# Nyström attention and two MoE layers on one core: the Newton turns of both head groups as one alternating product, and later scores

## The chip, the cores and the metric

One core of a Trainium2 chip. The metric is the device time of one execution in microseconds, on which PE (TensorE), DVE (VectorE), ACT (ScalarE), POOL (GpSimd), SP (SyncE) and the DMA queues work side by side. Each engine takes its instructions in order. The kernel before took 835.98 us (median of 3 runs, 835.73 to 837.34).

## The reference, cut to what matters

```python
B, H, S, D = q.shape            # 4, 8, 576, 64
m = 32
q_lm, k_lm = means of 18 rows of q, k          # 32 landmarks
A  = softmax(q @ k_lm.T / 8)                   # 576 x 32
Bm = softmax(q_lm @ k_lm.T / 8)                # 32 x 32
C  = softmax(q_lm @ k.T / 8)                   # 32 x 576
Z = Bm.T / (norm_1(Bm) * norm_inf(Bm) + 1e-06)
for _ in range(6):
    Z = 2 * Z - Z @ Bm @ Z                     # six Newton turns
x = A @ Z @ C @ v                              # per batch and head, then 2304 x 512
x = silu(x @ w_in) @ w_out                     # MoE1, d_ff 2048
xn = rms_norm(x) * rms_g
return (silu(xn @ w_gate) * (xn @ w_val)) @ w_out2   # MoE2, d_ff 1536
```

Everything is in fp32.

## The kernel before

**The order of the work.** Batch 0's attention comes first (`head`, in an order written out by hand). MoE1 then runs in 128 steps, 32 for each batch: two halves `hf` of 288 tokens, 16 blocks `f` of 128 hidden columns. The attention of batches 1 to 3 runs beside the MoE1 steps of the batch before it. MoE2 follows in three blocks of 768 tokens. A tile framework turns the order in which the code is traced, together with priorities, into one instruction list for each engine, with semaphores for the data and for the reuse of buffers.

**A step of MoE1.** `moe1_h` (L1018) makes `h`, 128 x 288, by six matmuls of 288 columns (products of a high and a low part), ACT makes `s` = silu(h), and ACT and DVE split `s` into the two parts of `hl` (L164, L165). `moe1_out` multiplies `hl` by `wo` into four accumulators `a` (L1038, 12 matmuls). Batch 0 takes unsplit `s` and `wor` in most of its steps (L1035, four fp32 matmuls). `retire` calls `moe1_out` three steps after its `h`. When a half is done, `moe1_sum` adds the four `a` to what is stored (`e`, L1063, DVE). During batch 0's steps DVE and ACT also turn `w_out` into its split form: `wor` (L189, L191) and `wo` (L165), 512 columns at a time. W' = `w_in` x the batch's small matrix is made in `wprime` (`pw`, L849).

**The attention of a batch.** The eight heads are two groups `g` of four heads, and a head has 32 of the 128 partitions. `attention(ap, b, g)` is a generator; each MoE1 step advances it by one `yield` (two in steps 20 to 31). Its stages are: loads of q and k; `landmarks`, a DVE sum of 128 x 1152 elements for each of `qT` and `kT` (L200); `scores` (16 matmuls, `pq` and `c`, each on a tile of 64 rows and 32 columns, L267); the maxima, exponentials and `bb` (Bm); `p1` (products and norms of Bm); `ct` (five transposes of C, L288); `pu` (C @ v, L295, 40 records of fp32); the six turns; `pl` (L828). Between them the query softmax `sa` is transposed to `sb` and split into `at` (`key_part`).

**A turn.** State `rt` is 128 x 96: 32 columns of R, made from Z Bm - I, and 64 of U. A turn needs R @ [R, U]:

```python
for it in range(6):
    pe_ = ps(f"pe_{n}_{it}", [P, 96])
    blocks(pe_[:, lo:], rt[:, 0:M], rt[:, lo:], start=True, stop=True)
    VE.tensor_copy(r2[:, 0:M], pe_[:, 0:M])
    VE.tensor_tensor(y, rt[:, M:], pe_[:, M:], op=ALU.add if it else ALU.subtract)
    yield
```

`blocks` (L273) issues four matmuls of 32 x 32 x 96 for the four heads, each on the tile (h, h) of the array: rows of head h, columns of head h. Both groups use the same four tiles. The last turn computes the 64 columns of U alone (`ud`). `head` gives batch 0 another form, in which a second product by plus or minus the identity adds U on PE and one copy empties the sum.

Group 0 runs LONE = 5 steps ahead of group 1. All PSUM tiles but the accumulators (`h`, scores, `p1`, `ct`, `pu`, `pe`, `pl`, `pw`) share four banks, `ps`. After batch 3's attention `att` is closed and pool `p2` opens, in which the first jobs of MoE2 (`pre`) work.

Of the kernel before, what the change touches and what calls it, by code (L numbers as in the profile page):

```python
# [10 lines left out]
F32 = mybir.dt.float32  # L11
F32R = mybir.dt.float32r
# [66 lines left out]
LOW = 9  # L79
LONE = 5  # L80


@with_exitstack
def nystrom_moe_kernel(ctx: ExitStack, tc: tile.TileContext, q, k, v, w_in, w_out, w_gate, w_val, w_out2, rms_g, out):
# [63 lines left out]
    def ps(name, shape=(P, 512)):  # L148
        return pr.tile(list(shape), F32, tag="r", name=name)
# [519 lines left out]
    def attention(ap, b, g):  # L669
# [40 lines left out]
        yield  # L710
        if b > 1:
            yield

        sa = ht("sa", [P, R, M])
        w1 = 320
        c1 = ps(f"c1_{n}", [P, w1])
        c2 = ps(f"c2_{n}", [P, S + M - w1])
        for hf, ci, lo, hi in ((0, c2, w1, S + M), (1, c1, 0, w1)):
            pq = ps(f"pq_{n}_{hf}", [P, HB])
            with tc.issue_after(h_mm[0].ins):  # L720
                for i in range(2):
                    scores(qT, kT, i, pq, ci, HB * hf, HB * hf + HB, lo, hi)
            VE.transpose(sa[:, 9 * hf:9 * hf + 9].rearrange("p r j -> p (r j)"), pq)
# [29 lines left out]
        VE.tensor_scalar(bb[:, 0], bb[:, 0], rc[:, 1:2], None, op0=ALU.mult)  # L753
        VE.transpose(bb[:, 1], bb[:, 0])
# [14 lines left out]
        ct = big("ct", [P, 5, P])  # L769
        tps = []  # L770
        for (i0, i1) in ((0, 4), (4, 5)):
            tp = ps(f"ct_{n}_{i0}", [VC[i0], i1 - i0, P])
            turn(tp, ec, i0, i1)
            tps.append((i0, i1, tp))
        yield
# [10 lines left out]
        VE.reciprocal(rc[:, 0:1], rc[:, 0:1])  # L786
        VE.tensor_scalar(rt[:, M:96], pu, rc[:, 0:1], ic, op0=ALU.mult, op1=ALU.mult)
        VE.tensor_tensor(sa, sa, msb, op=ALU.mult)
        yield
        keys = 0  # L790

        def key_part():
            nonlocal sb, at, keys
            if keys == 0:
                sb = big("sb", [P, S])
                VE.transpose(sb, sa.rearrange("p r j -> p (r j)"))
            elif keys == 1:
                at = xp.tile([P, 2, S], F32R, tag="x", name=f"at_{n}")
                AE.copy(at[:, 0], sb)
            elif keys == 2:  # L800
                VE.tensor_tensor(at[:, 1], sb, at[:, 0].bitcast(F32), op=ALU.subtract)
                at_t[b, g] = at
            keys += 1

        sb = at = None
        if g == 0:
            for _ in range(LONE):
                key_part()
                yield
        for it in range(6):  # L810
            pe_ = ps(f"pe_{n}_{it}", [P, 96])
            lo = 0 if it < 5 else M
            blocks(pe_[:, lo:], rt[:, 0:M], rt[:, lo:], start=True, stop=True)
            if it == 5:
                ud = mt("ud", [P, D])
            y = r2[:, M:] if it < 5 else ud
            if it < 5:
                VE.tensor_copy(r2[:, 0:M], pe_[:, 0:M])
            VE.tensor_tensor(y, rt[:, M:], pe_[:, M:], op=ALU.add if it else ALU.subtract)
            rt, r2 = r2, rt  # L820

            if it:
                key_part()
            yield

        hr = slice(64 * g, 64 * g + 64)
        pl = ps(f"pl_{n}", [P, 4, M])
        PE.matmul(pl[hr].rearrange(fl, h=4), ud, bbd.rearrange(fl, h=4), start=True, stop=True)  # L828
        if b not in lts:
            lts[b] = st.tile([P, 4, M], F32, tag="lt", name=f"lt_{b}", bufs=2)  # L830
        VE.tensor_copy(lts[b][hr], pl[hr])
        l_t[b, g] = True

# [320 lines left out]
    def store_out(e, row, last):  # L1154

        for h in range(2):
            y = slice(64 * h, 64 * h + 64)
            (SP, POOL, ACT)[h and last].dma_start(out=out[row + 64 * h:row + 64 * h + 64], in_=e[y])

# [84 lines left out]
    def out_tile(prev, n):  # L1244
# [9 lines left out]
        if f == NF2 - 1:  # L1254
            e = nslot(n, f"e2_{p}_{n}", [P, DM])
            last = 0 if p < NB2 // 2 - 1 else 1 + n // 5
            if last < 2:
                (DVE.tensor_copy if n % 2 else ACT.copy)(e, oacc[n])
            else:
                DVE.tensor_copy(e[:, :DM // 2], oacc[n][:, :DM // 2])  # L1260
                ACT.copy(e[:, DM // 2:], oacc[n][:, DM // 2:])
            store_out(e, (2 * p + j) * TB + t * P, last)

# [34 lines left out]
    VE.last, AE.last = Queue.last[DVE], Queue.last[ACT]  # L1298

    def behind(ins, fn):  # L1300
        with ExitStack() as es:
            for x in ins:
                es.enter_context(tc.issue_after(x.ins))
            fn()

# [54 lines left out]
    for i, (b, hf, f, c) in enumerate(steps):  # L1360
# [24 lines left out]
        if b == 0:  # L1385
# [129 lines left out]
```

## Time and profile before

| | us |
|---|---|
| median of 3 runs | 835.98 (835.73 to 837.34) |
| the profiled execution | 836.19 |
| its span in the trace | 834.1 |
| PE busy | 820.4 (98%) |
| DVE busy | 530.7 (64%) |
| ACT busy | 441.1 (53%) |

The span is what the trace shows between the first and the last instruction; 2.1 us of the execution lie around it. A row of a timeline gives the start in the span, the time from the first instruction's start to the last one's end, the line, the operation, what it writes and reads, tile and shape, and the number of records. An fp32 matmul leaves two records. The ends of matmuls overlap the next starts, so the time of a run is read from its start to the next row's start.

### The profile page before, as it was taken

The numbers are of one execution on the slowest core, as the hardware profiler recorded it, in microseconds if no ns is written. First come the engines' busy times: TensorE is split into PE (matmuls) and PEld (weight loads), VectorE is DVE, ScalarE is ACT, GpSimd is POOL, SyncE is SP. The second block draws the span as 40 slices with busy tenths as digits, with TensorE's granted clock in tenths as the row PEclk, the third lists the DMA queues.
The fourth block names the chain that finished last, engine by engine and source line by source line (L and its number), as shares of the span: only waits on it lengthen the run. The fifth ranks groups of instructions, "written<-read, shape, count | busy, mean of one in ns | idle before, by whom it ended". The sixth has DMA issues, their size and how long they took to land.

```text
span 834.1 us, 15381 instructions
## 1 busy us (share of the span) xinstructions
PE 820.4 (98%) x5912; PEld 734.1 (88%) x5912; DVE 530.7 (64%) x1141; ACT 441.1 (53%) x929; POOL 15.6 (2%) x45
## 2 busy tenths in 40 slices
PE   8899999999999999999999999999999999999997
PEld 5577677998898989999999999999999999999996
DVE  6988878786688767779735489543558433233323
ACT  4786755785668757775534456433245323233222
POOL 2200000000000000000000000000000000000001
PEclk9999999999999999999999999999999999999999
DMA  9989457458894679989975458678456557665542
GB/s 343 352 299 367 151 171 259 129 191 281 309 321 156 200 269 350 337 292 317 330 287 214 166 191 299 228 239 299 187 222 227 189 181 274 227 227 193 182 192 76
DMA packets 73320, 202.85 MB, mean 243 GB/s; under 512 B 6720, under 2 KB 34880, under 8 KB 69280
## 3 DMA queue, kind: packets, MB, share of 16 engines
q1 hardware_dynamic: 72928, 201.09, 67.2%
q8 instruction: 47, 0.77, 0.4%
q0 software_dynamic: 240, 0.66, 0.3%
q14 instruction: 25, 0.20, 0.1%
q10 hardware_dynamic: 80, 0.13, 0.0%
HBM read 149.29 MB, written 52.56 MB: 242 GB/s over the span
## 4 chain that ended last, share of the span: by engine, by line
PE 93%; ACT 2%; DMA 2%; DVE 1%; issue 1%; SPq 0%; POOL 0%; POOLq 0%; DVEq 0%; ACTq 0%
PE a L1038 21%; PE ga L1179 18%; PE o L1253 18%; PE h L1018 12%; PE gc L1179 9%; PE gb L1179 5%; PE a L1035 4%; PE pw L849 2%; DMA wor<-in_moe_w_out_dram 1%; PE pe L273 1%; DMA qT<-in_q_dram 1%; PE pu L295 1%; PE pq L267 1%; PE c L267 0%; PE ct L288 0%
## 5 line engine op out<-in xcount | busy, mean ns | idle before, releaser
L1038 PE MATMUL a<-hl,wo 128*128 128x288 f32 x1296 | 195.5, 299 | 1.2 <-DVE e L1063 1.2
L1038 PEld LDWEIGHTS a<-hl,wo 128*128 128x128 f32 x1296 | 177.8, 188 | 8.3 <-issue 2.9
L1253 PE MATMUL o<-oc,u 128*128 128x512 f32 x648 | 178.9, 394 | 0.0
L1179 PE MATMUL ga<-x,w 128*128 128x384 f32 x840 | 170.9, 338 | 0.0
L1179 PEld LDWEIGHTS ga<-x,w 128*128 128x128 f32 x840 | 151.3, 188 | 12.3 <-ACT a L200 0.2
L1253 PEld LDWEIGHTS o<-oc,u 128*128 128x128 f32 x648 | 119.4, 188 | 13.6 <-DVE u L165 0.3
L1018 PE MATMUL h<-at,wp 128*128 128x288 f32 x768 | 128.6, 302 | 0.0
L1018 PEld LDWEIGHTS h<-at,wp 128*128 128x128 f32 x768 | 109.6, 188 | 14.0 <-issue 5.9
L200 DVE TENSOR_TENSOR v<-u,gc 128x384 f32<-128x384 f32 x72 | 39.7, 551 | 122.6 <-PE gc L1179 122.1
L1179 PE MATMUL gc<-x,w 128*128 128x384 f32 x420 | 84.8, 336 | 0.0
L1025 ACT ACTIVATE s<-h 128x288 f32<-128x288 f32 x108 | 44.1, 412 | 74.8 <-PE h L1018 74.7
L1179 PEld LDWEIGHTS gc<-x,w 128*128 128x128 f32 x420 | 75.0, 188 | 2.9
L200 ACT COPY u<-ga 128x384 f32<-128x384 f32 x72 | 34.5, 480 | 72.9 <-PE ga L1179 72.6
L200 DVE TENSOR_TENSOR u<-z,v 128x384 f32<-128x384 f32 x72 | 40.1, 557 | 46.6 <-ACT z L200 45.5
L164 ACT CAST u<-u 128x384 fp32r<-128x384 f32 x72 | 37.0, 514 | 61.1 <-DVE u L200 61.0
L165 DVE TENSOR_TENSOR hl<-s,hl 128x288 fp32r<-128x288 f32 x108 | 49.1, 455 | 20.9 <-ACT hl L164 20.3
L165 DVE TENSOR_TENSOR u<-u,u 128x384 fp32r<-128x384 f32 x72 | 40.1, 557 | 26.3 <-ACT u L164 26.0
L200 ACT ACTIVATE z<-ga 128x384 f32<-128x384 f32 x36 | 17.7, 492 | 68.9 <-PE ga L1179 68.6
L164 ACT CAST hl<-s 128x288 fp32r<-128x288 f32 x108 | 46.6, 434 | 2.7
L1035 PE MATMUL a<-s,wor 128*128 128x288 f32 x160 | 42.6, 410 | 0.9 <-issue 0.9
L1179 PE MATMUL gb<-x,w 128*128 128x384 f32 x210 | 42.4, 336 | 0.0
L1035 PEld LDWEIGHTS a<-s,wor 128*128 128x128 f32 x160 | 29.1, 189 | 11.1 <-issue 3.3
(218 smaller groups left out, 931.1 us busy)
## 6 DMA issues: line engine op xcount, KB each, us to landing
w<-w7d SPq DMA_DIRECT2D x31, 1792.0 KB, 7.3
oc<-wod SPq DMA_DIRECT2D x32, 512.0 KB, 7.8
win<-wind SPq DMA_DIRECT2D x20, 512.0 KB, 5.3
w2d<-c SPq DMA_DIRECT2D x36, 256.0 KB, 2.5
fw<-w2d SPq DMA_DIRECT2D x12, 768.0 KB, 7.0
winr<-in_moe_w_in_dram SPq DMA_DIRECT2D x8, 1024.0 KB, 8.1
wor<-in_moe_w_out_dram SPq DMA_DIRECT2D x16, 512.0 KB, 9.8
w7d<-w7p SPq DMA_DIRECT2D x16, 512.0 KB, 5.1
```

The lines of the kernel that those rows point to most:

```text
L164: x = ACT.copy(dst[:, 0], src) if hi is ACT else hi.tensor_copy(dst[:, 0], src)
L165: return x, lo.tensor_tensor(dst[:, 1], src, dst[:, 0].bitcast(F32), op=ALU.subtract)
L200: self.last = getattr(self.eng, name)(*args, **kw)
L267: eng.matmul(out[32 * o:32 * o + 32], lm[y, i, S:], t[y, i, x0:x1], start=True, stop=True)
L273: eng.matmul(out[o], x[o], y[o], **kw)
L849: PE.matmul(pw[g][32 * i:32 * i + 32], lts[b][hr, i], win_t[i // 2, nb_][hr, i % 2], start=True, stop=True)
L1018: h_mm[0] = PE.matmul(ph, w[:, x, fo:fo + P], a[:, y, tk], start=i == 0, stop=i == 5)
L1025: ACT.activation(s, ph, AF.Silu)
L1035: PE.matmul(acc[d], w[:, y], hl, start=start, stop=stop)
L1038: PE.matmul(acc[d], w[:, x, y], hl[:, z], start=start and i == 0, stop=stop and i == 2)
L1179: mm[0] = PE.matmul(acc, w7[:, x, o, kk], xs[:, y, kk], start=start and n == 0, stop=stop and n == 5, skip_group_check=True)
L1253: PE.matmul(oacc[n], hls[j][:, x, t * P:(t + 1) * P], w[:, y], start=f == 0 and i == 0, stop=f == NF2 - 1 and i == 2)
```

## The change

1. `attend(ap, b)` takes the place of the two generators in the main loop and drives both. Group 0 starts `LONE[b]` steps ahead: 6, 8, 8 for batches 1, 2, 3. The extra yields before the scores are 0, 2, 1 (0, 1, 1 before). The turns begin when both groups have their `rt`.
2. A turn is one run of 16 matmuls, chained in order. The first eight multiply R by `rt` (96 columns, 64 in the last turn) and the other eight add U by plus or minus the identity (64 columns) into the same PSUM tile. The groups alternate: group 0 on tile (h, h), group 1 on tile (h, h^1). One DVE copy per group empties a turn. That makes 144 matmuls more and 36 DVE operations in place of 66 in three batches.
3. The 16 matmuls of a group's scores are chained as one run. `ct` comes before `p1` in another chain, behind the transpose of `bb`. `sb` and `at` are made before the turns, each at its own yield. `pl` of both groups is one run, and its copy has the sign.
4. The last output tile: DVE and ACT copy the halves into two tiles, which leave as 128 rows of 256 columns on POOL's and ACT's queues. Before, both wrote one tile, stored as 64 rows each by SP and ACT.

```diff
-LONE = 5
+LONE = (0, 6, 8, 8)
...
     class Queue:
         last = {}
-        def __init__(self, eng):
+        def __init__(self, eng, last=None):
             self.eng = eng
+            self.last = Queue.last if last is None else last
...
                     if self.eng in self.last:
                         es.enter_context(tc.issue_after(self.last[self.eng].ins))
+                        if self.last is not Queue.last:
+                            es.enter_context(tc.high_priority(offset=PU_PRIO))
...
-        if b > 1:
+        for _ in range((0, 0, 2, 1)[b]):
             yield
...
+        run = Queue(PE, {})
...
-                    scores(qT, kT, i, pq, ci, HB * hf, HB * hf + HB, lo, hi)
+                    scores(qT, kT, i, pq, ci, HB * hf, HB * hf + HB, lo, hi, run)
...
-        blocks(p1[:, 0:M], bb[:, 1], bb[:, 1], start=True, stop=True)
-        PE.matmul(p1[:, M:], ones_bd.rearrange(fl, h=4), bb.rearrange("p t j -> p (t j)"), start=True, stop=True)
+        run = Queue(PE, {})
+        tps = []
+        for (i0, i1) in ((0, 4), (4, 5)):
+            tps.append((i0, i1, ps(f"ct_{n}_{i0}", [VC[i0], i1 - i0, P])))
+        with behind([last]):
+            for i0, i1, tp in reversed(tps):
+                turn(tp, ec, i0, i1, run)
+            blocks(p1[:, 0:M], bb[:, 1], bb[:, 1], run, start=True, stop=True)
+            run.matmul(p1[:, M:], ones_bd.rearrange(fl, h=4), bb.rearrange("p t j -> p (t j)"), start=True, stop=True)
...
+    def attend(ap, b):
+        gens = [attention(ap, b, g) for g in range(NG)]
+        for _ in range(LONE[b]):
+            next(gens[0])
+            yield
+        while len([x for x in newton if x[0] == b]) < NG:
+            for gn in gens:
+                next(gn, None)
+            yield
+        rs = [list(x) for x in rts]
+        ins = [newton[b, g][1] for g in range(NG)]
         for it in range(6):
...
+            pes = [ps(f"pe_{b}_{g}_{it}", [P, 96]) for g in range(NG)]
+            run = Queue(PE, {})
+            for x0, x1, x, start in ((lo, 96, None, True), (M, 96, id32 if it else nid32, False)):
+                for h in range(4):
+                    for g, (rt, r2) in reversed(list(enumerate(rs))):
+                        y, z = slice(32 * h, 32 * h + 32), slice(32 * (h ^ g), 32 * (h ^ g) + 32)
+                        with behind(ins):
+                            run.matmul(pes[g][z, x0:x1], (rt[:, 0:M] if x is None else x)[y], rt[y, x0:x1], start=start, stop=not start, skip_group_check=True)
+            ins = []
+            for g, r in enumerate(rs):
+                if it == 5:
+                    r[1] = ap.tile([P, D], F32, tag="m", name=f"ud_{b}_{g}", bufs=7)
+                    ins.append(VE.tensor_copy(r[1], pes[g][:, M:]))
+                else:
+                    ins.append(VE.tensor_copy(r[1], pes[g]))
+                r.reverse()
+                next(gens[g], None)
             yield
...
+                e2 = nslot(n + 1, f"e2_{p}_{n}_1", [P, DM])
+                half = DM // 2
+                for eng, fn, t, x in ((POOL, DVE.tensor_copy, e, slice(0, half)), (ACT, ACT.copy, e2, slice(half, DM))):
+                    fn(t[:, x], oacc[n][:, x])
+                    eng.dma_start(out=out[row:row + P, x], in_=t[:, x])
...
-            gens = [attention(ap, nxt, g) for g in range(NG)]
+            gens = [attend(ap, nxt)]
...
-            run(gens[:1] if age < LONE and len(gens) == 2 else gens, 2 if FAST_AT <= i < 32 else 1)
-            age += 1
+            run(gens, 2 if FAST_AT <= i < 32 else 1)
```

How the instructions stand now, at three places. A row has the line, the operation, what it writes and reads (`pe_<group>_<turn>` before, the same names after; the last number counts buffers) and the shape.

PE in batch 2 before, where a turn of group 0 stands beside group 1's `p1` (named p) and `ct`:

```order
L1018 MATMUL h_0_14_2409<-at_0_1327,wp_3_1819 128x288 x3
L1018 MATMUL h_0_14_2409<-at_1_1516,wp_3_1819 128x288 x3
L273 MATMUL pe_0_1_2421<-rt_1_124 32x96 x4
L273 MATMUL p_2_1_2428<-bb_1_2344 32x32 x4
L760 MATMUL p_2_1_2428<-bb_1_2344,ones_bd 128x64
L1038 MATMUL a_0_0_0_1981<-hl_0_11_2303,wo_1684 128x288 x3
L288 MATMUL ct_1_0_2441<-ident,ec_1_2343 128x128 x4
L288 MATMUL ct_1_4_2446<-ident,ec_1_2343 64x128
L1038 MATMUL a_0_0_1_1982<-hl_0_11_2303,wo_1684 128x288 x3
```

PE in the same batch after the change, from group 1's `ct` to its p:

```order
L318 MATMUL ct_1_4_2454<-ident,ec_1_2381 64x128
L318 MATMUL ct_1_0_2453<-ident,ec_1_2381 128x128 x4
L1061 MATMUL a_0_0_0_2012<-hl_0_11_2340,wo_1722 128x288 x3
L1061 MATMUL a_0_0_1_2013<-hl_0_11_2340,wo_1722 128x288
L318 MATMUL p_2_1_2452<-bb_1_2382 32x32 x4
L318 MATMUL p_2_1_2452<-bb_1_2382,ones_bd 128x64
L1061 MATMUL a_0_0_1_2013<-hl_0_11_2340,wo_1722 128x288 x2
L1061 MATMUL a_0_0_2_2014<-hl_0_11_2340,wo_1722 128x288 x3
```

The turn has left this place, and matmuls of `a` stand between `ct` and p. The turns of batch 2 come after both groups' `pu`, one in each MoE1 step.

DVE in batch 1 before, where group 1's scores are emptied (`sa_1`):

```order
L191 SCALAR_TENSOR_TENSOR wor_926<-wos_1170,wor_926 128x512
L165 TENSOR_TENSOR hl_1_0_1187<-s_1_0_1185,hl_1_0_1187 128x288
L200 SCALAR_TENSOR_TENSOR rt_0_123<-p_1_0_1190,ic_0_1198,id_102 128x32
L200 STREAM_TRANSPOSE sa_1_1210<-pq_1_0_1213 128x288
L200 STREAM_TRANSPOSE sa_1_1210<-pq_1_1_1223 128x288
L189 SCALAR_TENSOR_TENSOR wor_949<-wor_949 128x512
L200 TENSOR_REDUCE ms_1_1238<-sa_1_1210 128x18
```

DVE in batch 1 after the change, at the same `wor_926`:

```order
L191 SCALAR_TENSOR_TENSOR wor_926<-wos_1169,wor_926 128x512
L165 TENSOR_TENSOR hl_1_0_1186<-s_1_0_1184,hl_1_0_1186 128x288
L200 TENSOR_SCALAR ic_0_1204<-cr_0_1202 128x1
L200 STREAM_TRANSPOSE sb_0_1290<-sa_0_1022 128x576
L200 RECIPROCAL ic_0_1204<-ic_0_1204 128x1
L189 SCALAR_TENSOR_TENSOR wor_949<-wor_949 128x512
L200 SCALAR_TENSOR_TENSOR rt_0_123<-p_1_0_1189,ic_0_1204,id_102 128x32
L200 TENSOR_REDUCE kT_1_1045<-kT_1_1045 128x2x32
L191 SCALAR_TENSOR_TENSOR wor_949<-wos_1242,wor_949 128x512
L165 TENSOR_TENSOR wo_1247<-wor_629,wo_1247 128x512
L200 STREAM_TRANSPOSE sa_1_1215<-pq_1_0_1218 128x288
```

The sum of `kT_1`, on which the scores of group 1 rest, and the transpose `sb_0` have come in between `hl_1_0` and the first `sa_1` transpose. Before, `kT_1` stood ahead of `wor_887`, right behind the transpose of `bb_0`; there `qT_1` stands after the change.

PE in batch 1 after the change, from the end of turn 3 to the start of turn 4:

```order
L318 MATMUL pe_0_3_1564<-rt_1_124,id_102 32x64
L1061 MATMUL a_1_1_2_1391<-hl_1_3_1361,wo_1247 128x288 x2
L1061 MATMUL a_1_1_3_1392<-hl_1_3_1361,wo_1247 128x288 x2
L318 MATMUL pe_1_4_1585<-rt_0_125 32x96
L1061 MATMUL a_1_1_3_1392<-hl_1_3_1361,wo_1247 128x288
L1061 MATMUL a_1_1_0_1389<-hl_1_4_1417,wo_1305 128x288 x3
L318 MATMUL pe_0_4_1584<-rt_0_123 32x96
```

Turn 4 has its first matmul (group 1) apart from the other fifteen, with four matmuls of `a` between them. Turn 2 is cut in the same way, with one matmul between.

## Rows read from the trace of the kernel before

**Rows 1.** The page: busy time by engine, and the chain that ended last by engine.

```profile
PE 820.4 (98%) x5912; PEld 734.1 (88%) x5912; DVE 530.7 (64%) x1141; ACT 441.1 (53%) x929; POOL 15.6 (2%) x45
...
PE 93%; ACT 2%; DMA 2%; DVE 1%; issue 1%; SPq 0%; POOL 0%; POOLq 0%; DVEq 0%; ACTq 0%
```

**Rows 2.** Three stretches (us) with busy time, instructions, granted clock and DMA.

```profile
88.00:106.00 18.00, 16.18 (x156) 11.54 (x155) 17.68 (x46) 14.40 (x30) 0.41 (x2) 1.00 0.27 97
130.00:310.00 180.00, 179.93 (x1755) 158.72 (x1754) 135.18 (x317) 121.75 (x263) 1.60 (x4) 1.00 0.69 232
400.00:420.00 20.00, 19.78 (x130) 19.03 (x129) 13.06 (x29) 10.37 (x25) 0.00 (x0) 1.00 1.00 353
```

**Rows 3.** PE's timeline in batch 1: start us, us, engine, line, operation, count.

```profile
109.64 0.53 PE L273 MATMUL pe<-rt 32*32 32x96 f32 x16
110.10 0.66 PE L1038 MATMUL a<-hl,wo 128*128 128x288 f32 x3
110.69 0.37 PE L273 MATMUL pe<-rt 32*32 32x96 f32 x8
110.99 0.40 PE L1038 MATMUL a<-hl,wo 128*128 128x288 f32 x1
...
113.72 2.26 PE L1038 MATMUL a<-hl,wo 128*128 128x288 f32 x15
115.91 0.37 PE L273 MATMUL pe<-rt 32*32 32x96 f32 x8
```

**Rows 4.** PE's timeline in batch 0: one group's turn with the identity part.

```profile
20.11 0.37 PE L309 MATMUL pe<-rt 32*32 32x96 f32 x8
20.30 0.29 PE L309 MATMUL pe<-rt,nid 32*32 32x64 f32 x8
20.41 0.34 PE L309 MATMUL pe<-rt 32*32 32x96 f32 x8
```

**Rows 5.** PE's timeline in batch 2: first and last of ten visits of pe.

```profile
175.62 0.37 PE L273 MATMUL pe<-rt 32*32 32x96 f32 x8
...
204.18 0.31 PE L273 MATMUL pe<-rt 32*32 32x64 f32 x8
```

**Rows 6.** PE's timeline: scores of batch 2, and of batch 3's group 1.

```profile
138.55 0.69 PE L267 MATMUL pq<-qT,kT 64*32 64x288 f32 x8
139.17 0.40 PE L1038 MATMUL a<-hl,wo 128*128 128x288 f32 x1
139.50 0.45 PE L267 MATMUL c<-kT,qT 64*32 64x288 f32 x4
...
140.66 0.53 PE L1038 MATMUL a<-hl,wo 128*128 128x288 f32 x2
...
164.55 0.43 PE L267 MATMUL pq<-qT,kT 64*32 64x288 f32 x1
...
165.82 0.66 PE L1038 MATMUL a<-hl,wo 128*128 128x288 f32 x3
...
256.36 0.69 PE L267 MATMUL pq<-qT,kT 64*32 64x288 f32 x8
...
259.75 0.74 PE L267 MATMUL c<-kT,qT 64*32 64x320 f32 x8
```

**Rows 7.** Timelines of DVE and PE in batch 1; in brackets idle time, releaser.

```profile
87.70 1.31 DVE L200 TENSOR_REDUCE kT<-kT 128x64 f32<-128x1152 f32 x1
...
93.95 0.69 DVE L191 SCALAR_TENSOR_TENSOR wor<-wos,wor 128x512 int32<-128x512 int32 x1
94.56 0.45 DVE L165 TENSOR_TENSOR hl<-s,hl 128x288 fp32r<-128x288 f32 x1
...
93.66 0.43 PE L267 MATMUL pq<-qT,kT 64*32 64x288 f32 x1
...
103.72 0.53 PE L1038 MATMUL a<-hl,wo 128*128 128x288 f32 x2 [1.19 <-DVE e L1063]
```

**Rows 8.** ACT's timeline at the end of the span.

```profile
829.04 0.37 ACT L1261 COPY e<-o 128x256 f32<-128x256 f32 x1 [0.58 <-DVE e L1260]
```

More of the change, by code (lines that the diff above doesn't have):

```diff
@@ L260, in nystrom_moe_kernel, with behind @@
     spare = {}
+    def behind(ins):
+        es = ExitStack()
+        for x in ins:
+            es.enter_context(tc.issue_after(x.ins))
+        return es
     def scores(qT, kT, i, a, c, lo, hi, lo2, hi2, eng=PE):
@@ L753, in attention @@
         VE.tensor_scalar(bb[:, 0], bb[:, 0], rc[:, 1:2], None, op0=ALU.mult)
-        VE.transpose(bb[:, 1], bb[:, 0])
+        last = VE.transpose(bb[:, 1], bb[:, 0])
         bbd = mt("bbd", [P, 4, M])
@@ L769, in attention @@
         ct = big("ct", [P, 5, P])
[L770 to L774, printed above, removed]
         yield
@@ L786, in attention @@
         VE.reciprocal(rc[:, 0:1], rc[:, 0:1])
-        VE.tensor_scalar(rt[:, M:96], pu, rc[:, 0:1], ic, op0=ALU.mult, op1=ALU.mult)
+        newton[b, g] = bbd, VE.tensor_scalar(rt[:, M:96], pu, rc[:, 0:1], ic, op0=ALU.mult, op1=ALU.mult)
         VE.tensor_tensor(sa, sa, msb, op=ALU.mult)
         yield
[L790 to L809, printed above, removed]
+        sb = big("sb", [P, S])
+        VE.transpose(sb, sa.rearrange("p r j -> p (r j)"))
+        yield
+        at = xp.tile([P, 2, S], F32R, tag="x", name=f"at_{n}")
+        AE.copy(at[:, 0], sb)
+        yield
+        VE.tensor_tensor(at[:, 1], sb, at[:, 0].bitcast(F32), op=ALU.subtract)
+        at_t[b, g] = at
+    newton = {}
+    def attend(ap, b):
+        gens = [attention(ap, b, g) for g in range(NG)]
+        for _ in range(LONE[b]):
+            next(gens[0])
+            yield
+        while len([x for x in newton if x[0] == b]) < NG:
+            for gn in gens:
+                next(gn, None)
+            yield
+        rs = [list(x) for x in rts]
+        ins = [newton[b, g][1] for g in range(NG)]
@@ L822, in attention @@
-            if it:
-                key_part()
-            yield
[L826 to L832, printed above, removed]
+            pes = [ps(f"pe_{b}_{g}_{it}", [P, 96]) for g in range(NG)]
+            run = Queue(PE, {})
@@ new lines, in attend @@
+            ins = []
[7 more added lines that the diff above has]
+                next(gens[g], None)
+            yield
+        lts[b] = st.tile([P, 4, M], F32, tag="lt", name=f"lt_{b}", bufs=2)
+        pls = [ps(f"pl_{b}_{g}", [P, 4, M]) for g in range(NG)]
@@ L834, in wprime @@
+        run = Queue(PE, {})
+        for g in reversed(range(NG)):
+            hr = slice(64 * g, 64 * g + 64)
+            pl = pls[g]
+            with behind(ins):
+                run.matmul(pl[hr].rearrange(fl, h=4), rs[g][0], newton[b, g][0].rearrange(fl, h=4), start=True, stop=True)
+            VE.tensor_scalar(lts[b][hr], pl[hr], -1.0, None, op0=ALU.mult)
+            l_t[b, g] = True
     def wprime(b, nb_, prio=0):
@@ L1157, in store_out @@
             y = slice(64 * h, 64 * h + 64)
-            (SP, POOL, ACT)[h and last].dma_start(out=out[row + 64 * h:row + 64 * h + 64], in_=e[y])
+            (SP, POOL)[h and last].dma_start(out=out[row + 64 * h:row + 64 * h + 64], in_=e[y])
     nx = {}
@@ L1258, in out_tile @@
                 (DVE.tensor_copy if n % 2 else ACT.copy)(e, oacc[n])
+                store_out(e, row, last)
             else:
-                DVE.tensor_copy(e[:, :DM // 2], oacc[n][:, :DM // 2])
-                ACT.copy(e[:, DM // 2:], oacc[n][:, DM // 2:])
-            store_out(e, (2 * p + j) * TB + t * P, last)
+                e2 = nslot(n + 1, f"e2_{p}_{n}_1", [P, DM])
[3 more added lines that the diff above has]
+                    eng.dma_start(out=out[row:row + P, x], in_=t[:, x])
     def pg(name, tag):
@@ L1298, in nystrom_moe_kernel @@
     VE.last, AE.last = Queue.last[DVE], Queue.last[ACT]
[L1300 to L1304, printed above, removed]
     todo = [(b, n if b else quarter(n)) for b in range(B) for n in range(4)]
@@ L1389, in nystrom_moe_kernel @@
             if i in CONV_AT:
-                behind((*cuts, *after), lambda: finish(jobs.pop(CONV_AT[i])))
+                with behind((*cuts, *after)):
+                    finish(jobs.pop(CONV_AT[i]))
             if i in KEEP_AT:
@@ L1394, in nystrom_moe_kernel @@
         if 0 <= i - SPLIT_AT < NF:
-            behind(cuts, lambda: split_wout(i - SPLIT_AT))
+            with behind(cuts):
+                split_wout(i - SPLIT_AT)
         if todo and todo[0][0] >= max(b, 1) and ready(todo[0][0]) and wpfree and not (jobs and todo[0][0] > b):
```

11 lines of the change are left out of this document (1 added, 10 removed).

## Prediction

> **What bounds the kernel now.** I read the page first: PE is busy 98% of the span and makes 93% of the chain that ended last [rows 1]. So only two things count: PE time that is added or saved, and new waits of PE. Next I read the table by stretches for where PE still waits [rows 2]. From 130 to 310 us, where batches 2 and 3 do their attention beside MoE1, PE is busy 179.93 of 180 us and DVE 135.18 (75%): there saved PE time is saved time, as long as DVE stays ahead. From 88 to 106 us, in batch 1, it is the reverse: DVE is busy 17.68 of 18 us and PE 16.18; that stretch belongs to DVE. The granted clock is 1.00 in all three stretches, so nothing below comes from the clock. Then I read PE's own timeline around the small matmuls for the price of a burst [rows 3], batch 0 for the form of a turn that the change brings to the other batches [rows 4], and the places of the Newton turns and of the scores [rows 5, 6].
>
> **The price of a burst.** Between 113.72 and 115.91 there are 15 matmuls of `a` and one burst boundary, between 110.10 and 110.69 three and one boundary [rows 3]. Twelve matmuls make the difference of 2.19 - 0.59 = 1.60 us, so one takes 0.133, and 0.59 - 3 x 0.133 = 0.19 us is lost at each visit of a burst of small tiles, over and above the burst itself. A turn of one group takes 0.30 (110.69 to 110.99), of both groups back to back 0.46 (109.64 to 110.10) [rows 3]. The second group costs 0.16 because it stands on the same four tiles as the first.
>
> **Newton turns.** The new turn has 16 matmuls on eight tiles, 8 of 96 columns and 8 of 64 that add U by an identity. Batch 0 has this form for one group: 0.19 us from the 96-column part to the identity part, 0.11 from there to the next turn [rows 4]. Ends of the range: if the groups' tiles overlap wholly, 0.30 + 0.11 = 0.41; if the two groups stand one after another, 0.46 + 2 x 0.11 = 0.68. I take 0.43, near the low end, because the scores of [rows 6] run on eight tiles at a time: 32 records of about 300 columns take 1.27 us. The last turn (64 columns) I take as 0.37. The Trainium skill, "TensorEngine Tiling (Array Packing)", Instruction Overhead, gives each matmul some 60 cycles beyond its columns. By that the 64-column part would be (64 + 60) / (96 + 60) of 0.19, 0.15 us, a turn 0.47 and 18 turns 0.7 us dearer than I count; the trace differs, since 0.11 to 0.19 is even less than 64 to 96.
>
> *Batch 2* has its turns now in ten visits, of which [rows 5] show the first and the last: eight turns of one group alone at 0.30 and two pairs at 0.46. Three of the eight share a visit with other small work (p, pu, pl), which leaves seven visits of their own; the one with pu is cut in two by it, a turn's start more (0.3). That is 8 x 0.30 + 2 x 0.46 + 0.3 + 7 x 0.19 = 4.95, some 0.1 less for the 64 columns of the two last turns. Afterwards: 5 x 0.43 + 0.37 + 6 x 0.19 = 3.7. The two pl visits become one: -0.4 by a boundary and the start of a visit (the 0.19 and about 0.2). But p, which rode along with a turn, now goes alone (+0.2), and the fence on PE shows that ct of group 1 and p stand apart, one boundary more (+0.2). Sum: **-1.2 us**, between -0.5 and -1.7.
> *Batch 3* has six pairs now; six turns of 0.43 in place of 0.46 give **-0.15** (up to +1.3 with turns of 0.68).
> *Batch 1* has nine visits now; the order shows six turns afterwards, but two of them with their first matmul apart from the other fifteen, so eight visits: -0.2.
> DVE has 36 operations in place of 66. I cost that at nothing in batches 2 and 3: PE does not wait there now, so there is nothing to give back.
>
> **Scores.** In one run 16 matmuls take 1.27 us (164.55 to 165.82). Group 0 of batch 2 has them in two runs: 0.62 (138.55 to 139.17) and 1.16 (139.50 to 140.66), 0.51 more, and a boundary of 0.19 [rows 6]. In one run: **-0.7**. Group 1 of batch 3 has three runs, the first and the last in [rows 6], of 0.62, 0.65 and 0.67: 0.67 and two boundaries more, **-1.05**. The other two groups of these batches are in one run already. The ends are nothing and these full amounts; I take the full amounts, since PE is busy on both sides.
>
> **Batch 1, the part that costs.** Group 1 starts six steps behind group 0 in place of five. The fence on DVE shows what that does: the sum `kT_1`, 1.31 us, which stands at 87.70 now, goes behind `wor_926`, `hl_1_0`, the key transpose of group 0 (which moves up), half of `wor_949` and `rt_0`. qT's sum of the same size takes the old place. `wor_926` ends at 93.95 + 0.69 = 94.64 [rows 7]. Behind it: hl 0.4, a transpose of 576 columns 0.7, a 512-column step 0.6 (93.95 to 94.56), three small ones 0.3, the sum 1.3 [rows 7], the transpose and the small ones estimates from these rows. `kT_1` is done at about 98.0, and PE's scores of group 1, which begin at 93.66 now, begin 4.3 us later. PE has two steps of `a` to do in that time, the second of which waits for `wor_926` itself, and then stands still. It does not lose all of it, for it stands still now too: 1.19 us at 103.72 for the first `e` sum of DVE [rows 7]. Between `kT_1` and that sum DVE's new order has 15 rows: three 512-column steps (1.8), four of 576 or 2 x 288 columns (2.8), two hl (0.8), maxima, biases and rt (1.4). That makes 6.8 and the sum itself 0.4: the wait at `a` ends at about 105.2, 1.5 later than now. By then PE has done one `h` more (six matmuls, 0.8). Net **+0.7**. Then the turns: each copy of a turn stands on DVE between hl and wo steps of 0.45 and 0.6, and PE meets the next turn after one or half a step; I take 0.3 for two of the five, +0.6. With the -0.2 from above batch 1 is **+1.1**, between 0 (all of it made good before batch 2) and +4.3.
>
> **The rest.** In the turns and in ct before p of batches 2 and 3 I take +0.3 for new short waits (0 to 1.2, the longest wait of this kind in [rows 7]). Batch 3's pl comes three steps later, so the pool of MoE2's first jobs opens three steps later; they now run beside the last steps of MoE1, and from 400 to 420 PE waits for only 0.22 us of 20 [rows 2]. DVE and ACT are not full there (13.06 and 10.37 of 20), so I take +0.4, from 0 to 1.2 as above. At the end ACT waits 0.58 us for DVE's half of the last tile [rows 8], in the same tile; with its own tile it needn't. But the halves now leave in two stores of 128 rows, one of them on POOL's queue behind POOL's previous store: -0.4 to +0.3, I take 0.
>
> **Sum:** -1.2 - 0.15 - 0.7 - 1.05 + 1.1 + 0.3 + 0.4 = **-1.3 us**. The profiled execution took 836.19 us (span 834.1), so 834.9 against it; it lies 0.2 above the median 835.98, so I forecast **834.7**. A measurement of this kernel can tell 0.2%, 1.7 us, from no change: faster is below 834.3, slower above 837.7.
>
> **Rivals.**
> *Nothing waits.* DVE makes up batch 1 in its later idle time, and the transition costs nothing: batch 1 -0.2, the rest 0, so -3.3 and **832.7**. For it: DVE falls to 75% after 130 us. Against: PE is busy in all of it, so time that PE loses in batch 1 stays lost.
> *Batch 1 belongs to DVE to its end (slower).* One mechanism: PE waits for `kT_1`, and the work behind it (e sums, the softmax of group 1, p, rt) moves by the same amount, since the DVE queue is full. Then the 4.3 us are lost whole, and the five turns after the first each wait 0.3: 4.3 + 1.5 - 0.2 = 5.6 in place of 1.1, **839.2**. It decides once batch 1 loses more than 4.1 us (the other parts give 2.4 back, and 1.7 is the bound). For it: 17.68 of 18 us busy. Against: the 1.19 us of PE's idle time, and the `h` steps ahead of the wait. The Trainium skill, "TensorEngine Tiling (Array Packing)", PSUM Bottleneck, asks for PSUM to be emptied by ScalarE and VectorE both once packed tiles have sped TensorE up; by it the copies, which all stay on VectorE, would be the limit. The trace bears that out for 88 to 106 us alone.
> *The tiles don't overlap.* Turns of 0.68 in place of 0.43, 18 times (0.25 x 18 = 4.5): **839.2**. Against: the score runs [rows 6].
> *The change moves waits only.* PE's saving in batches 2 and 3 is taken back by DVE and ACT, whose work per step stays the same: **836.0**. For it: DVE carries 75%, not less. Against: PE waits 0.07 us in 180.
>
> **How the numbers follow.** Forecast 0.50, with a range of its own from 833.4 to 836.2; nothing waits 0.24; batch 1 0.10; tiles 0.05; waits only 0.11. The forecast lies 0.4 us above the bound of faster: of its 0.50 I count 0.18 as faster, 0.31 as no change and 0.01 as slower. Faster: 0.24 + 0.18 = 0.42. Slower: 0.10 + 0.05 + 0.01 = 0.16. No change: 0.31 + 0.11 = 0.42. The range from 832.3 to 838.0 holds the forecast, the last rival and most of the first; it leaves out most of the two slow cases (0.13) and some 0.06 below, where batch 1 loses nothing and the turns take 0.41.
>
> **What would show it.** In the new profile: runs of 16 matmuls of pe of 0.4 to 0.45 us, and 0.6 or more if the tiles don't overlap. Score runs of 1.27 us, once per group. PE idle before the scores of group 1 in batch 1, with DVE's kT sum as its releaser, and all of PE's work behind batch 1 about 1 us late; it would be 5 us late by the slow rival, and early by the first. Between 130 and 310 us PE still idle for less than 0.5 us. I am wrong if that stretch has waits of some us, or if PE's waits between 88 and 130 us add up to under 1.8 or over 6 us.

## The result: 1.3% slower

| | before | changed |
|---|---|---|
| median, us | 835.89 (4 runs, 835.73 to 837.34) | 846.60 (4 runs, 846.0 to 848.37) |
| the profiled execution, us | 836.19 | 846.0 |
| its span, us | 834.1 | 843.9 |

The ratio is 1.0128, with a 95% interval from 1.0109 to 1.0147. The forecast was 834.7 us with a range from 832.3 to 838.0, so the result lies far outside on the slow side.

The page of the profile of the changed kernel, against [rows 1]:

```profile
PE 819.6 (97%) x6200; PEld 737.5 (87%) x6200; DVE 528.6 (63%) x1111; ACT 440.3 (52%) x929; POOL 16.2 (2%) x46
...
PE 88%; DMA 5%; DVE 3%; ACT 2%; SPq 1%; issue 1%; POOL 0%; POOLq 0%; ACTq 0%; DVEq 0%
```

PE is busy 0.8 us less than before, with 288 more records. The span grew all the same, so PE waits more. The chain tells for what: DMA and DVE now hold 8% of it in place of 3%. The table by stretches, in the columns of [rows 2], says where:

```profile
88.00:106.00 18.00, 14.90 (x146) 11.31 (x145) 17.76 (x41) 12.28 (x24) 0.28 (x1) 1.00 0.21 77
130.00:310.00 180.00, 179.87 (x1971) 162.76 (x1978) 134.89 (x300) 123.69 (x267) 1.60 (x4) 1.00 0.70 234
400.00:420.00 20.00, 16.45 (x110) 15.62 (x108) 12.45 (x28) 9.82 (x23) 0.00 (x0) 1.00 0.99 344
```

From 130 to 310 us nothing is wrong: PE idles 0.13 us. From 400 to 420 us, where MoE1 ends and MoE2 begins, PE idles 3.55 us of 20 where it idled 0.22.

To split the difference I read starts of rows in PE's timeline of each profiled execution: the first `h` of MoE1, the third W' run (`pw`) of batch 1 and of batch 2, the first product of MoE2 (`ga`), PE's last end, the end of the span. The stretches between them, in us (the last two columns are experiments below; each column is one profiled execution):

| stretch | before | changed | difference | LONE 5 in batch 3 | p first, old tail |
|---|---|---|---|---|---|
| start to first `h` | 32.45 | 33.02 | +0.57 | 33.85 | 32.47 |
| to W' of batch 1 | 98.09 | 98.62 | +0.53 | 98.56 | 98.13 |
| to W' of batch 2 | 90.64 | 88.46 | -2.18 | 88.45 | 88.09 |
| to MoE2 | 188.54 | 189.51 | +0.97 | 188.49 | 188.66 |
| MoE2 to PE's end | 418.82 | 428.07 | **+9.25** | 418.66 | 418.62 |
| to the end of the span | 5.55 | 6.23 | +0.68 | 5.89 | 5.53 |

The changed kernel begins MoE2 at 409.61, the one before at 409.73. Up to there the two are level, and the loss comes right after. PE's timeline there (in brackets idle time and releaser):

```profile
414.31 1.31 PE L1202 MATMUL ga<-x,w7p 128*128 128x384 f32 x6 [1.07 <-ACT u L200]
...
416.19 1.33 PE L1202 MATMUL ga<-x,w7p 128*128 128x384 f32 x6
423.95 2.29 PE L1202 MATMUL gc<-x,w7p 128*128 128x384 f32 x6 [6.43 <-DVE v L200]
```

Two waits, 7.5 us. The 6.43 us are put down to `v` on DVE, an operation of half a microsecond. The chain of waits of the stretch from 380 to 430 us shows what is behind it:

```profile
397.01 10.79 DMA w7d<-w7p
407.82 0.52 ACT w7p L164
...
411.36 0.70 SPq L954
...
416.58 5.21 DMA fw<-w2d
...
421.88 1.11 DVE t L942 x3
...
423.35 0.56 DVE v L200
```

The names: the jobs of `pre`, and `late` from unit 8 on, turn MoE2's weights into their split form one unit (a slice `f`) after another: a raw load `fw` (L933), sums `t` on DVE (L942), splits into `w7p` on ACT and DVE (L164, L165), stores to `w7d` by SP (L954). `w7p` is one buffer. The splits of the last unit in front of unit 8 (f = 0) waited until 407.82 for the buffer's earlier store, so its own stores went out on SP's queue at 409 to 412. Behind those stores stand the stores of MoE1's last sums (`x2T`, L1090) and a load of MoE2's tokens (`xb`, L1115), and behind these unit 8's raw load. SP before, then SP after:

```profile
389.46 1.25 SPq L910 DMA_DIRECT2D fw<-w2d  x1
...
400.09 1.72 SPq L931 DMA_DIRECT2D w7d<-w7p  x2
...
411.58 1.01 SPq L910 DMA_DIRECT2D fw<-w2d  x1
```

```profile
386.75 1.19 SPq L933 DMA_DIRECT2D fw<-w2d  x1
...
408.96 3.11 SPq L954 DMA_DIRECT2D w7d<-w7p  x4
412.12 1.34 SPq L1090 DMA_DIRECT2D x2T<-e  x1
413.51 2.53 SPq L1090 DMA_DIRECT2D x2T<-ex  x3
416.08 0.46 SPq L1115 DMA_DIRECT2D xb<-x2T  x1
416.58 0.50 SPq L933 DMA_DIRECT2D fw<-w2d  x1
```

Before, the load at 389.46 is unit 8's and the one at 411.58 is unit 9's. After, the load at 386.75 belongs to the unit in front (f = 0, split last), and unit 8's is the one at 416.58, 27 us later than before. The order has turned too: before, unit 8's load went out ahead of the last stores of f = 0 (400.09); now it stands behind them and behind the stores of MoE1's sums. DVE before and after shows why PE cared:

```profile
405.43 0.76 DVE L919 TENSOR_TENSOR t<-fw 128x256 f32<-128x256 f32 x2
406.10 0.89 DVE L919 TENSOR_TENSOR t<-fw,t 128x256 f32<-128x256 f32 x2
...
415.48 0.55 DVE L200 TENSOR_TENSOR v<-u,gc 128x384 f32<-128x384 f32 x1 [0.44 <-ACT u L200]
```

```profile
421.88 0.76 DVE L942 TENSOR_TENSOR t<-fw 128x256 f32<-128x256 f32 x2 [7.35 <-DMA fw<-w2d]
422.56 0.88 DVE L942 TENSOR_TENSOR t<-fw,t 128x256 f32<-128x256 f32 x2
423.35 0.55 DVE L200 TENSOR_TENSOR v<-u,gc 128x384 f32<-128x384 f32 x1
```

In both kernels unit 8's four sums stand ahead of the first `v` in DVE's order. Before, their load had landed long ago and they were done at 407. After, DVE stood 7.35 us at the first of them, with `v` queued behind, though nothing needed unit 8 yet. That is 7.5 us of waits, against 0.22 before; the clock adds the rest of the 9.25:

```profile
424.00:426.00 2.00, 2.00 (x6) 2.00 (x7) 0.56 (x1) 0.51 (x1) 0.00 (x0) 0.50 0.85 328
...
428.00:430.00 2.00, 2.00 (x11) 1.85 (x10) 0.82 (x2) 0.89 (x2) 0.00 (x0) 0.94 0.85 323
```

The granted clock was 0.50, the 1.2 GHz level, from 424 to 428 us, right behind the long idle stretch: about 2 us of work not done.

### The profile page after: what moved, and what is told of

The parts are those of the page before. It is cut to its first block, busy times and chain, and to the rows that moved or that the text cites. A ratio compares the mean times of both kernels' runs of the same rounds, so it can differ in the third digit from the quotient of the medians.

```text
span 843.9 us, 15909 instructions
## 1 busy us (share of the span) xinstructions
PE 819.6 (97%) x6200; PEld 737.5 (87%) x6200; DVE 528.6 (63%) x1111; ACT 440.3 (52%) x929; POOL 16.2 (2%) x46
## 4 chain that ended last, share of the span: by engine, by line
PE 88%; DMA 5%; DVE 3%; ACT 2%; SPq 1%; issue 1%; POOL 0%; POOLq 0%; ACTq 0%; DVEq 0%
PE a L1061 18%; PE o L1276 18%; PE ga L1202 18%; PE h L1041 12%; PE gc L1202 9%; PE gb L1202 4%; PE a L1058 4%; PE pw L872 2%; DMA winr<-in_moe_w_in_dram 2%; DMA w7d<-w7p 1%; PE pe L318 1%; DMA win<-wind 1%; DMA fw<-w2d 1%; DMA kT<-in_k_dram 1%; PE pu L301 1%; PE pq L318 1%
## 5 line engine op out<-in xcount | busy, mean ns | idle before, releaser
L164 ACT CAST u<-u 128x384 fp32r<-128x384 f32 x72 | 37.0, 514 | 66.9 <-DVE u L200 66.9
L165 DVE TENSOR_TENSOR hl<-s,hl 128x288 fp32r<-128x288 f32 x108 | 48.7, 451 | 25.8 <-ACT hl L164 24.0
L165 DVE TENSOR_TENSOR u<-u,u 128x384 fp32r<-128x384 f32 x72 | 40.0, 556 | 27.1 <-ACT u L164 26.8
L164 ACT CAST hl<-s 128x288 fp32r<-128x288 f32 x108 | 46.8, 433 | 2.6
```

Of the source, the lines that this page charges most:

```text
L164: x = ACT.copy(dst[:, 0], src) if hi is ACT else hi.tensor_copy(dst[:, 0], src)
L165: return x, lo.tensor_tensor(dst[:, 1], src, dst[:, 0].bitcast(F32), op=ALU.subtract)
```

## The experiments

Theory: the loss comes from the pool `p2`. With LONE = 8 in batch 3 its attention ends three steps later, `p2` opens three steps later, and the weight units with it. Rival causes were the Newton turns, the scores and batch 1. Every run computes the whole reference.

**The kernel before, with its pool opened three steps later.**

```diff
-        if nxt == B and not gens and p2 is None:
+        wait_p2 += nxt == B and not gens
+        if wait_p2 > 3 and p2 is None:
```

> The kernel before with one thing added: pool p2, in which MoE2's first weight jobs work, opens three MoE1 steps later, as the change makes it. Theory A (the late pool makes the loss): the last jobs' splits and stores fall behind the end of MoE1, PE waits some 7 us for DVE's v near 416 us, and the time is 843 to 847. Theory B (another part of the change makes the loss, such as its turns, its scores or the new order on DVE): three steps don't matter, 835 to 837.

Measured: 848.36 us, ratio 1.0144 [1.0127, 1.0162]. PE's waits (total, times, longest):

```profile
PE gc L1179 <- DVE v L200: 6.8, 1, 6.8
...
PE ga L1179 <- ACT u L200: 1.1, 1, 1.1
```

The late pool alone, with the old turns and the old scores, makes the same two waits, as theory A says (the time is 1.4 us above its range). MoE2 to PE's end is 428.67 against 428.07.

**The change, with LONE = 5 in batch 3.**

```diff
-LONE = (0, 6, 8, 8)
+LONE = (0, 6, 8, 5)
```

> The change with LONE[3] = 5 in place of 8, so that batch 3's attention ends, and the pool opens, in the step in which they did before. Theory A: the wait near 416 us is gone, and the other parts show alone: 0.9 lost in batch 1, 1 to 2 saved in batches 2 and 3, so 835 to 838. Theory B: 844 to 847, as with the whole change.

Measured: 835.78, ratio 0.999 [0.998, 1.000]. Both waits are gone and MoE2 takes 418.66. From both sides the pool's date is shown to carry the loss. The rest of the change, with the new tail, can hardly be told from no change.

**The change, with more units prepared in each step.**

```diff
-PRE_STEPS, PRE_RATE = 12, 2.5
+PRE_STEPS, PRE_RATE = 12, 2.75
```

> The change with the rate of the first weight jobs raised from 2.5 to 2.75 a step, the pool as late as in the change. Theory A in its sharper form (what counts is that the jobs are done by the end of MoE1, not where batch 3's turns stand): 835 to 838. Theory B, or a loss that comes from the turns' later place itself: 844 to 847.

Measured: 837.11, ratio 1.0007 [0.9998, 1.0017]. The pool opens as late as in the change, and MoE2 takes 418.62. So here a late pool costs nothing that can be told from no change, once the units behind it are done in time.

**One and two steps late, in the kernel before** (`wait_p2 > 1` and `wait_p2 > 2` in the diff of the first experiment).

> The kernel before with the pool opened one step later. In DVE's order unit 8's sums stand ahead of the first v with x tiles between, as before. Theory (there is a step or so of slack): 836 to 837.5. Rival (each late step costs its third of the 10 us): 839 to 841.

> The kernel before with the pool opened two steps later. Here the framework puts unit 8's sums behind the first two v on DVE. Theory (the 6.8 us wait needs both: a late load and sums ahead of v): no such wait, 836.5 to 840, less than the run with three steps by 6 us or more. Rival (each late step costs its third): 842 to 844.

Measured: 838.77 (1.0024 [1.0015, 1.0033]) and 839.64 (1.003 [1.0021, 1.004]). With the 11.6 us of three steps the series is 2.1, 2.9, 11.6: no slope but a step. Both runs lose something ahead of MoE2: from W' of batch 2 to MoE2 they take 189.66 and 190.37 us in place of 188.54, with a new wait of `a` for the copies `e` and `ex` of MoE1's sums, 0.6 and 1.4 us. So the slack of a step that was expected at one step isn't there. But with unit 8's load out at 392.29 MoE2 takes 418.66 at one step and loses nothing. At two steps the load goes out at 422.16, later than in the change, and the longest wait for `v`, with what DVE did ahead of it, is this:

```profile
PE gb L1179 <- DVE v L200: 1.2, 1, 1.2
```

```profile
433.79 0.76 DVE L919 TENSOR_TENSOR t<-fw 128x256 f32<-128x256 f32 x2 [1.78 <-DMA fw<-w2d]
```

There the scheduler put unit 8's sums behind the first three `v` in DVE's order. DVE stood only 1.78 us at them, and the `v` behind them made PE wait 1.2. The jump is where the sums stand ahead of the first `v` and their load is late.

**The change, with unit 8's sums (and those of the units behind it) forced behind the DVE instruction traced last before them.**

```diff
             if k < 2:
-                sums(i, 2 * k)
-                sums(i, 2 * k + 1)
+                with tc.issue_after(VE.last.ins):
+                    sums(i, 2 * k)
+                    sums(i, 2 * k + 1)
```

> The change with the pool as late as it made it, and one order more: the DVE sums of weight unit 8 (and of the units behind it), which stand ahead of the first v in DVE's queue, come behind the DVE work of MoE2 that was written before them. Theory A2: PE's wait of 6.4 us comes from these sums alone; they wait for a load that stands on SP's queue behind the late stores, and DVE can't go past them. Then that wait goes, 1 us of the other wait stays: 836.5 to 839.5. Rival A1: the late splits and stores themselves, or the loads behind them on SP's queue, hold PE however DVE is ordered: 843 to 847.

Measured: 840.74, ratio 1.0051 [1.0036, 1.0066], between the ranges of the two theories. The wait of 6.4 us is gone, a smaller one has come (PE's waits, then the stretch in which the clock had been 0.50):

```profile
PE o L1277 <- DMA oc<-wod: 2.4, 1, 2.4
...
PE ga L1203 <- ACT u L200: 1.1, 1, 1.1
```

```profile
424.00:426.00 2.00, 1.44 (x7) 1.33 (x8) 0.00 (x0) 0.00 (x0) 0.00 (x0) 1.00 1.03 421
```

MoE2 takes 422.11: 6.0 of the 9.25 us are the sums ahead of `v` and the clock behind them. The other 3.3 are the wait for `oc`, which the first `o` needs and which SP loads behind the late stores too, and the 1.1, which stays (0.2 before). So theory A2 holds for the 6.4 us, and the loads behind the late stores hold PE too, as A1 says.

**The kernel before, with the new tail alone** (the last tile in two tiles, on POOL's and ACT's queues).

> The kernel before with the change's form of the last output tile alone (two tiles, two stores of 128 rows on the queues of POOL and ACT). In the profile of the change the ACT copy still waits for DVE's half, and from PE's last matmul to the end of the span it is 0.7 us longer than before. Theory: the new stores are the slower ones, +0.4 to +1.0. Rival, as I predicted: 0, between -0.4 and +0.3.

Measured: 837.06, ratio 1.0009 [1.0000, 1.0018]. From PE's end to the span's end it is 6.13 us against 5.55. The change with LONE = 5 and the old tail answers from the other side:

> The second run's kernel (LONE[3] = 5) with the last output tile in its form of before. Theory (the new tail costs 0.3 from PE's last matmul to the end of the span): 0.2 to 0.5 faster than the second run, 835.3 to 836.0 where before is 836.4 to 836.8. Rival (the tail is hidden in the scatter): no difference.

Measured: 835.00, ratio 0.9981 [0.9972, 0.999], with 5.45 us behind PE's end. The new tail costs about half a microsecond by the traces, and less by the medians of the run with the tail alone (0.3).

**LONE = 5 in batch 1 as well**, against LONE = 6 there.

```diff
-LONE = (0, 6, 8, 5)
+LONE = (0, 5, 8, 5)
```

> The change with LONE = (0, 5, 8, 5): batch 3 as in the second run, and group 1 of batch 1 five steps behind group 0 as before, so that the sum kT_1 takes its old place on DVE. Theory (the 0.9 us that batch 1 loses come from kT_1 behind a full DVE queue): PE's scores of group 1 come some 3 us earlier, and the stretch from 78 to 132 us is 0.5 to 1.2 us shorter than in the second run; 834.6 to 835.5. Rival (DVE is full whatever its order, and the same work has to be done before the first e sum): no difference, within 0.3.

Measured: 836.52, ratio 0.9999 [0.9989, 1.0008]; batch 1 took 99.06 us to its W', against 98.56, so the theory missed. Group 1's scores start at 95.11 and PE then waits for DVE's `e` sum 1.42 us. The date of `kT_1` alone is not what batch 1 costs: the time goes into one wait or the other.

**p before `ct` in the chain** (on top of LONE = 5 in batch 3 and the old tail).

```diff
         with behind([last]):
-            for i0, i1, tp in reversed(tps):
-                turn(tp, ec, i0, i1, run)
             blocks(p1[:, 0:M], bb[:, 1], bb[:, 1], run, start=True, stop=True)
             run.matmul(p1[:, M:], ones_bd.rearrange(fl, h=4), bb.rearrange("p t j -> p (t j)"), start=True, stop=True)
+            for i0, i1, tp in tps:
+                turn(tp, ec, i0, i1, run)
```

> The kernel of the run beside it, and p1 before ct in their chain, as it was before the change. Theory (in batch 1 group 0's p waits 1.1 us for ACT's s because ct's two tiles took the banks first, where ct waited 0.6 before): 0.3 to 0.6 faster than the run beside it, by the stretch of batch 1. Rival (whichever is last in the chain waits for the same s): no difference.

Measured: 833.87, ratio 0.9967 [0.9955, 0.9979]. This beats the kernel before by 0.33% and, by the medians, the change by 1.5%. PE in batch 1, with `ct` first (LONE = 5 in batch 3), then with p first (the first `h` starts 1.38 us earlier in this profile):

```profile
92.33 0.26 PE L318 MATMUL p<-bb 32*32 32x32 f32 x8 [1.07 <-ACT s L1045]
```

```profile
89.73 0.26 PE L318 MATMUL p<-bb 32*32 32x32 f32 x8
...
91.43 0.30 PE L318 MATMUL ct<-ident,ec 128*64 128x128 f32 x1 [0.62 <-ACT s L1045]
```

p no longer stands behind the wait, and DVE gets the norms of Bm earlier. Batch 1 takes 98.13 us in place of 98.77 (the same kernel with `ct` first), batch 2 88.09 in place of 88.52. That is more than the 0.3 to 0.6 expected. The kernel before took 98.09 in batch 1, so with p first nothing is left there of what the change lost. Which of the small waits in between gave how much, the traces don't tell.

**Both groups on the same four tiles** (the change with LONE = 5 in batch 3, group 1 on (h, h) too).

```diff
-                        y, z = slice(32 * h, 32 * h + 32), slice(32 * (h ^ g), 32 * (h ^ g) + 32)
+                        y, z = slice(32 * h, 32 * h + 32), slice(32 * h, 32 * h + 32)
```

> The second run's kernel with group 1's turns on the tiles (h, h), on which group 0's stand, in place of (h, h^1). Theory (eight tiles overlap, four don't): a turn takes 0.55 to 0.68 us in place of 0.44, 18 turns, so +2.0 to +4.3, 837.8 to 840. Rival (the turn is held by the issue of 32 records, or by what lies around it): no difference, 835.3 to 836.3.

Measured: 840.08, ratio 1.0043 [1.0026, 1.006], 4.3 us over LONE = 5, just above the range of the theory. A turn on eight tiles (the change, batch 2), then on four:

```profile
187.94 0.39 PE L318 MATMUL pe<-rt 32*32 32x96 f32 x16
188.13 0.32 PE L318 MATMUL pe<-rt,nid 32*32 32x64 f32 x16
188.38 1.85 PE L1061 MATMUL a<-hl,wo 128*128 128x288 f32 x12
```

```profile
189.03 0.55 PE L318 MATMUL pe<-rt 32*32 32x96 f32 x16
189.38 0.44 PE L318 MATMUL pe<-rt,nid 32*32 32x64 f32 x16
189.75 1.85 PE L1061 MATMUL a<-hl,wo 128*128 128x288 f32 x12
```

From start to the next row's start a turn takes 0.44 against 0.72 us. So the two groups overlap more on eight tiles than on the same four.

**Scores without the chain** (the change with LONE = 5 in batch 3; `run` left out of the call of `scores`).

> The second run's kernel with the scores not chained in one run, each matmul placed by the framework. Theory (a run cut in two costs 0.7, in three 1.05): +1 to +2.5 us, if the framework cuts the runs as it did before; 836.8 to 838.3. Rival (the cut runs were filled with other work, so that nothing is saved by closing them): 835.3 to 836.3.

Measured: 836.24, ratio 0.9996 [0.9987, 1.0005]. Inconclusive: the scheduler left five of the six score runs whole without a chain, and cut batch 3's group 1 in three pieces (from 256.58, 258.19 and 260.33 us), as LONE = 5 has it with the chain (from 256.17, 257.90 and 259.92). So the number of cuts, which the run was to change, did not change, and the stretch from batch 2's W' to MoE2 is 188.51 against 188.49.

## Why the prediction was wrong, step by step

**The step that failed** is in "The rest": "the pool of MoE2's first jobs opens three steps later; they now run beside the last steps of MoE1 ... I take +0.4, from 0 to 1.2". It measured +9.25. I looked at DVE's and ACT's idle share in that stretch [rows 2] and asked whether they had room. They had: DVE is busy 12.45 of 20 us after the change, no more than the 13.06 before. What decided was order, as the chain of waits above shows it. `w7p`, one buffer, held the splits until its store had landed; SP's in-order queue then held unit 8's load behind the late stores and the stores of `x2T`; DVE's in-order queue held `v` behind sums that waited for this load. None of the three was in the sum, and the bound of 1.2 was taken from a wait in batch 1 [rows 7], which has nothing to do with this place. That the sums ahead of `v` hold PE, and that all goes with the date of the units, was tried by runs; the buffer and the place of the load on SP's queue are read from the trace, and no run changed one of them alone.

**The turns, right.** 0.43 was forecast, 0.44 measured, with rows like [rows 4]. The rival that the tiles don't overlap (0.68) is refuted by it, and the four-tile run shows what it would have cost: 0.72 a turn, and 4.3 us for the whole kernel where 4.5 was forecast. By the prediction's estimate from the overhead of some 60 cycles that the Trainium skill gives each matmul ("TensorEngine Tiling (Array Packing)", Instruction Overhead), a turn would have taken 0.47. The trace gives 0.44, nearer to the 0.43 from its own rows.

**Batch 2, right.** Turns and scores were -1.2 and -0.7, together -1.9; measured -2.18. The scores stand in one run of 1.27 us, as forecast. No run parts the two terms. The +0.3 for short waits did not come: PE idles 0.13 us from 130 to 310.

**Batch 3, right in its own part, but a wait was missed.** -0.15 and -1.05 make -1.2; measured +0.97. A W' run there waited for its load:

```profile
309.82 1.09 PE L872 MATMUL pw<-win,lt 64*32 64x512 f32 x16
310.84 1.06 PE L1041 MATMUL h<-at,wp 128*128 128x288 f32 x6
...
314.54 2.22 PE L872 MATMUL pw<-win,lt 64*32 64x512 f32 x16 [1.07 <-DMA win<-wind]
316.69 1.06 PE L1041 MATMUL h<-at,wp 128*128 128x288 f32 x6
```

SP's rows for that load, before and after:

```profile
302.45 4.43 SPq L860 DMA_DIRECT2D win<-wind  x4
```

```profile
307.81 3.95 SPq L883 DMA_DIRECT2D win<-wind  x4
```

Before, two W' runs lie four steps apart (304.96 and 315.76) and the load is issued at 302.45. With batch 3's attention three steps later they stand in successive steps, and the load goes out at 307.81. The second run lost 1.07 before it and took 2.15 in place of 1.02: 2.2 us in all. Without these, batch 3 has -1.2, which is the forecast. It is the same mistake: `pl` was moved by three steps, and I priced what it computes, not the loads that hang on its date. That score runs made these -1.2 is argued and not shown: with LONE = 5 the run is cut in three again and the stretch saves 0.05, which fits, but there the place of the whole attention moved too, and the unchained run has the same three pieces.

**Batch 1, the dates right, the cost not.** +1.1 was forecast, +0.53 measured (0.46 to 0.85 in the six profiles whose batch 1 is that of the change). Its dates can be checked row by row: `kT_1` ends at 98.22 (98.0 forecast), the scores begin at 98.32 (4.3 later than 93.66 makes 97.96), `a` goes on behind the `e` sum at 105.35 (105.2), with no wait in front of it. PE idles 1.07 us before these scores, which the view puts down to "issue"; the idle time ends 0.1 us behind `kT_1`. PE's waits from 88 to 130 us add up to 3.1, inside the 1.8 to 6 that were set. But the sum itself does not hold. Turns 2 and 4 were cut, as the order showed, yet PE did not wait for a copy, so the +0.6 is not there. And PE waited for p, which now stands behind `ct`; before, it had waited 0.63 for `ct` (before, then after):

```profile
91.36 0.30 PE L288 MATMUL ct<-ident,ec 128*64 128x128 f32 x1 [0.63 <-ACT s L1022]
```

```profile
91.63 0.26 PE L318 MATMUL p<-bb 32*32 32x32 f32 x8 [1.06 <-ACT s L1045]
```

Waits for `ct` before p were priced for batches 2 and 3 alone. With p first batch 1 takes 98.13, with `kT_1` at its old place (LONE = 5 in batch 1) 99.06, and before the change 98.09. So the loss goes with the new order of the chain, and an earlier `kT_1` does not take it away. That +0.53 lies inside the range of this term is in part luck. The slow rival for batch 1 (5.6 us) is refuted by the 0.53. The Trainium skill, "TensorEngine Tiling (Array Packing)", PSUM Bottleneck, says that the copies out of PSUM may become the limit once tiling has sped TensorE up. With all copies of the turns on VectorE, PE idles 0.13 us from 130 to 310 us, so the trace shows no such limit there.

**The tail, wrong in small.** Forecast 0, measured +0.68 in the change, +0.58 with the tail alone. A tile of its own does not free ACT from DVE: it waits 0.57 us, where [rows 8] have 0.58:

```profile
838.17 0.37 ACT L1288 COPY e<-o 128x256 f32<-128x256 f32 x1 [0.57 <-DVE e L1288]
838.55 0.57 POOL L1289 DMA_DIRECT2D out_dram<-e  x1
838.57 0.37 ACTq L1289 DMA_DIRECT2D out_dram<-e  x1
```

What the two copies still share is the accumulator that they read, and that this is the cause was not tried. The separate tile wins nothing, and the span ends later behind PE's last matmul.

**No rival named the place.** All four moved the time by waits of batch 1, tiles or nothing. A fifth was in sight: a moved date of `p2` and the chain of stores and loads behind it. None of the signs of being wrong looked behind 310 us. The chance of slower, 0.16, came from batch 1 and the tiles alone, but for 0.01 of the forecast's own scatter.

## What to carry to other kernels

When a change moves the date of a stage, follow what is traced behind that date to its end: each load's place on its queue, each one-buffer tile and the store that frees it, each instruction on an in-order engine that will stand at the load with other work behind it. An engine with idle time is no cover for work that is late, since a late operand blocks the queue whatever the engine's share of busy time: DVE, busy 12.45 of 20 us, stood 7.35 us at one load. And when a packet of edits is level or worse, run its side effects alone: the new turns, and in batch 2 turns and scores together, were worth about what the rows said, and a single number, how far ahead batch 3's group 0 starts, hid it.

## What the runs showed of the hardware

The granted clock was 0.50 behind PE's 6.43 us of idle time and back at 0.94 in 428 to 430 us. In the run with unit 8's sums behind, whose longest wait there was 2.4 us, it stayed 1.00.

The head is not as steady as the rest. The change and the run with PRE_RATE = 2.75 differ only in a rate that acts from batch 3 on, yet in 32 to 34 us, where MoE1's first `h` starts, the clock was 1.00 in the profiled execution of that run and 0.58 in that of the change:

```profile
32.00:34.00 2.00, 2.00 (x26) 1.55 (x11) 0.74 (x4) 1.06 (x5) 0.00 (x0) 1.00 1.03 418
```

```profile
32.00:34.00 2.00, 2.00 (x15) 1.69 (x8) 0.97 (x5) 1.29 (x6) 0.00 (x0) 0.58 1.03 416
```

MoE1's first `h` started between 32.45 and 34.41 us in the fourteen profiled executions. Up to 2 us between two profiles lie there, so stretches are better compared from a start inside each.
